# High weights of the last 64 inputs times low inputs: from eight full matmuls per output to seven and a share in two pairs of 64-row matmuls

## The chip, the cores and the metric

The kernel runs on one core of one Trainium2 chip. The metric is the device time of one execution in microseconds. Times and traces of the kernel before come from the hardware profiler; all times below are microseconds (us) unless marked ns.

## The reference: what is computed

Three parts follow each other, all in 32-bit floats. First a gated linear attention (mLSTM) over 2 batches, 8 heads, 768 steps and head size 40; its output, 1536 tokens of 320 numbers, goes into a gated layer and then into a two-layer one:

```
C = f_stab * C + i_stab * outer(v_t, k_t);  n = f_stab * n + i_stab * k_t
y_t = sigmoid(o_t) * (C q_t) / max(|n . q_t|, 1)          # 1536 x 320 over all steps
xn  = x / rms(x) * rms_g                                  # first layer's input
g   = xn @ w_gate;  val = xn @ w_val                      # 320 -> 1536 each
x   = (g * sigmoid(g) * val) @ w_out                      # 1536 -> 320
h   = x @ w_in                                            # 320 -> 2048
out = leaky_relu(h, 0.01) @ w_out2                        # 2048 -> 320
```

The weights are handed in as 64-bit floats and turned into 32-bit ones on the chip.

## The kernel before, in words

**Numbers as high and low parts.** TensorE (PE) multiplies in a shortened 32-bit format (fp32r). So each number of an input X and of a weight W is kept as a high part, rounded to that format, and a low part, the rest; a product is high times high, plus high times low, plus low times high. The input of a layer has 320 rows: two blocks of 128 and a last one of 64. The tile `X` holds six planes of 1536 token columns: planes 0, 1 and 2 are the high parts, 3, 4 and 5 the low ones. Planes 2 and 5 hold the last 64 inputs twice, in partitions 0 to 63 and again in 64 to 127. The weight tile `wA` of one block `f` has five planes: 0 and 1 high, 2 and 3 low, and plane 4 for the last 64 inputs, with the high weights in one half of the partitions and the low ones in the other. The halves alternate with the block's number (`weight_r`): an even block has its high weights in partitions 0 to 63, an odd one in 64 to 127.

**One output** of an up layer is 128 output features by 384 or 512 tokens, in one of the eight PSUM banks. The function `up` makes it with eight matmuls of 128 rows. The seventh is plane 4 times plane 2, which gives high times high and low times high for the last 64 inputs; the eighth is plane 4 times plane 5, which gives high times low, and low times low with it.

**Stages.** Attention runs in 12 tiles of 128 tokens (T = 0 to 11). Behind it the first layer's feature blocks 0 to 7 run in four token groups of 384 (`GA`), and blocks 8 to 11 and the whole second network in three groups of 512 (`GB`). `U.g.f.h` makes one output of block f for group g (h = 0 is the gate, tile name `g`, h = 1 the value, tile name `v`); T (tanh, ScalarE, ACT), E and M (products, VectorE, DVE), S (copy to the high part, ACT) and L (low part, DVE) follow; `D` and `DW` multiply down into 320 outputs (tiles `xa`, `xw`), `K` and `KW` add the result to `x2`, `FX` folds and `X` splits `x2` into the planes again. `H.g.f` makes an output of the second network (tile `h`), `R` applies the leaky relu (ACT, tile `u`), S and L split it, `O` multiplies down (tile `oa`), `OK` and `dO` keep and store. In attention `qk` makes the scores (tile `s`): for each head pair two matmuls of 40 rows, one in partitions 0 to 39 and one in 64 to 103, into two banks. `av`, `inn` and `kv` write column slices, `tp` transposes.

**What sets the order.** Nothing is scheduled when the kernel is built. The string `ORDER` lists the steps, `play` calls them in turn, and each engine and the DMA queue of SyncE (SP) run their instructions in that order; a step waits only where it needs data or a buffer. PSUM banks come from four tags of two banks each: `gv` (gates; outputs h with odd f), `s` (values of blocks 8 to 11; scores), `o` (outputs h with even f; xw of the third slice) and `acc` (sums). `a`, `r` and `b` convert weights on DVE and ACT, `id` are matmuls on constants that keep PE busy in attention.

Of the kernel before, what the change touches and what calls it, by code (L numbers as in the profile page):

```python
# [50 lines left out]
rec.0 wA.1 a.1 rec.1 r.2 dq.2 a.1 yr.0 id.1 mask.3.0 arg.3.0 r.2 id.1 r.2 qk.2 th.1 st.0 y1.1 de.2 dA.2.6 eq.2 ux.1.2
co.1.1.2 cv.1.1.2 cv.0.2.6 sq.0 y2.0.0 yr.1 wA.2 kv.1 dgb p.2.0 av.2.0 arg.2.1 y2.0.1 p.2.1 y2.0.2 k.2 sq.1 y2.1.0 a.2
y2.1.1 a.1 xn.0 a.2 arg.3.1 a.1 dq.3 qk.3 p.3.1 dq.4 cb.0 wB.1 a.2 xc.0 b.1 dsl y2.1.2 th.2 a.2 dr.2.6 da.4 mask.4.1
wA.4 xn.1 av.2.1 inn.2 y1.2 xc.1 id.1 st.1 abs.2 id.1 id.1 id.1 p.3.0 rec.2 tp.0 id.1 b.1 tp.1 dn.3 yr.2 dr.1.2
mask.4.0 dc.1.2 a.4 sq.2 b.1 y2.2.0 kv.2 xh.1 wR.3 th.3 de.3 dE.2.6 k.3 b.1 id.1 xh.0 xl.0 av.3.0 co.1.2.6 cv.1.2.6
xl.1 cb.1 y2.2.1 y2.2.2 r.3 qk.4 eq.3 av.3.1 inn.3 dv.1.2 xn.2 arg.4.0 xc.2 tp.2 abs.3 r.3 r.3 c.3 rec.3 dn.5 kv.3 a.4
xh.2 arg.4.1 xl.2 U.0.1.1 p.4.0 k.5 y1.3 da.5 a.4 st.3 U.0.1.0 cb.3 p.4.1 th.5 T.0.1 dn.4 th.4 mask.5.0 wA.3 yr.3 sq.3
a.4 E.0.1 mask.5.1 a.3 arg.5.1 dc.2.6 de.4 r.3 arg.5.0 y2.3.0 a.3 eq.4 M.0.1 av.4.0 av.4.1 inn.4 dq.5 qk.5 y2.3.1 y1.4
p.5.1 U.0.0.0 p.5.0 T.0.0 E.0.0 dv.2.6 U.0.0.1 M.0.0 da.6 mask.6.1 arg.6.1 de.5 wB.0 abs.4 dq.6 a.3 rec.4 mask.6.0
av.5.0 av.5.1 S.0.1 eq.5 y2.3.2 yr.4 S.0.0 inn.5 kv.5 abs.5 b.0 xn.3 rec.5 b.0 sq.4 y2.4.0 y2.4.1 arg.6.0 qk.6 L.0.1  # L60
p.6.1 U.0.2.0 p.6.0 U.0.2.1 T.0.2 E.0.2 c.2 y1.5 dq.7 b.0 c.5 st.5 qk.7 yr.5 y2.4.2 c.4 cb.5 sq.5 a.3 k.4 kv.4 id.1
xc.3 tp.3 xh.3 y2.5.0 y2.5.1 dq.8 xn.4 da.7 xc.4 M.0.2 wB.2 U.0.3.0 st.4 cb.4 y2.5.2 c.6 L.0.0 xn.5 xl.3 tp.4 xh.4
xl.4 U.0.3.1 S.0.2 xc.5 T.0.3 tp.5 xh.5 de.6 dn.6 av.6.0 E.0.3 xl.5 av.6.1 wB.3 M.0.3 L.0.2 eq.6 inn.6 abs.6 wA.5 b.0
b.3 U.1.0.0 T.1.0 E.1.0 U.1.0.1 M.1.0 U.1.1.0 da.8 U.1.2.0 b.3 mask.7.0 arg.7.0 p.7.0 dn.7 av.7.0 mask.7.1 arg.7.1
p.7.1 av.7.1 k.7 S.0.3 b.2 L.0.3 de.7 b.2 eq.7 S.1.0 b.2 inn.7 L.1.0 b.2 b.3 b.3 wB.4 rec.6 T.1.2 E.1.2 mask.8.1 a.5
da.9 mask.9.0 mask.9.1 b.4 qk.8 a.5 th.7 T.1.1 th.6 y1.6 D.0.0.2 E.1.1 D.0.0.1 K.0.0.1 U.1.2.1 M.1.2 U.1.1.1 arg.8.1
p.8.1 M.1.1 mask.8.0 D.0.0.0 S.1.1 L.1.1 yr.6 S.1.2 a.5 wA.7 U.1.3.0 a.5 L.1.2 arg.8.0 b.4 p.8.0 de.9 dq.9 kv.7 T.1.3
E.1.3 k.6 eq.9 kv.6 st.6 arg.9.1 cb.6 U.1.3.1 M.1.3 abs.7 a.7 dn.8 a.7 U.0.5.0 T.0.5 E.0.5 sq.6 qk.9 K.0.0.0 av.8.0
de.8 S.1.3 L.1.3 p.9.1 a.7 k.8 eq.8 av.8.1 rec.7 c.7 inn.8 th.8 abs.8 a.7 rec.8 U.0.4.0 wA.6 a.6 a.6 T.0.4 a.6 y2.6.0
y2.6.1 U.0.5.1 M.0.5 E.0.4 dq.10 dn.9 y1.8 yr.8 th.9 K.0.0.2 D.1.0.0 b.4 sq.8 U.0.4.1 st.7 a.6 U.0.6.1 M.0.4 wA.10  # L70
wB.6 b.6 b.6 S.0.4 L.0.4 y2.6.2 b.4 xn.6 U.0.6.0 cb.7 da.10 D.1.0.2 K.1.0.0 y1.7 D.1.0.1 k.9 T.0.6 mask.10.1 arg.9.0
wB.9 y2.8.0 yr.7 y2.8.1 E.0.6 p.9.0 M.0.6 y2.8.2 av.9.0 av.9.1 inn.9 b.6 K.1.0.2 kv.9 wB.5 b.5 b.5 abs.9 rec.9 c.9
st.9 S.0.5 kv.8 qk.10 mask.10.0 S.0.6 L.0.5 L.0.6 b.5 b.5 b.9 U.1.6.0 T.1.6 xn.8 xc.8 dn.11 c.8 st.8 xc.6 E.1.6 y1.9
yr.9 U.0.7.0 T.0.7 U.0.7.1 E.0.7 M.0.7 b.6 tp.6 cb.8 wB.7 b.7 b.7 b.7 b.7 K.1.0.1 tp.8 U.1.6.1 S.0.7 L.0.7 U.1.4.0
D.0.1.2 xh.6 M.1.6 xl.6 T.1.4 a.10 da.11 E.1.4 sq.7 y2.7.0 sq.9 y2.7.1 D.0.1.0 y2.7.2 mask.11.1 K.0.1.0 U.1.4.1 S.1.6
L.1.6 xh.8 xl.8 arg.10.0 y2.9.0 U.1.7.0 arg.10.1 p.10.1 T.1.7 E.1.7 D.0.1.1 dn.10 U.1.5.0 M.1.4 y2.9.1 p.10.0 xn.7
xc.7 y2.9.2 S.1.4 L.1.4 U.1.7.1 a.10 tp.7 M.1.7 de.10 eq.10 arg.11.1 cb.9 K.0.1.2 dq.11 qk.11 mask.11.0 xh.7 xl.7
T.1.5 av.10.0 av.10.1 E.1.5 inn.10 abs.10 rec.10 th.10 y1.10 yr.10 U.1.5.1 M.1.5 arg.11.0 S.1.5 S.1.7 U.2.2.0 L.1.5
T.2.2 L.1.7 U.2.1.0 T.2.1 E.2.1 sq.10 p.11.1 E.2.2 de.11 xn.9 D.1.1.0 K.1.1.0 U.2.1.1 M.2.1 U.2.2.1 S.2.1 M.2.2
U.2.0.0 L.2.1 T.2.0 E.2.0 D.1.1.2 K.1.1.2 wA.9 U.2.0.1 M.2.0 D.1.1.1 y2.10.0 S.2.2 y2.10.1 K.0.1.1 K.1.1.1 b.9 th.11  # L80
eq.11 S.2.0 L.2.0 U.2.3.0 T.2.3 L.2.2 U.2.3.1 xc.9 tp.9 xh.9 p.11.0 av.11.0 av.11.1 wR.5 E.2.3 M.2.3 S.2.3 y2.10.2
inn.11 L.2.3 D.2.0.1 abs.11 rec.11 y1.11 yr.11 sq.11 K.2.0.1 D.2.0.0 xn.10 D.2.0.2 y2.11.0 xc.10 xl.9 y2.11.1 y2.11.2
xn.11 xc.11 tp.10 tp.11 close U.2.4.0 a.10 a.10 wA.8 a.8 b.9 a.8 wR.4 xh.10 U.2.5.0 xl.10 wA.12 T.2.4 E.2.4 U.2.4.1
M.2.4 xh.11 xl.11 S.2.4 L.2.4 b.9 a.8 a.8 T.2.5 E.2.5 U.2.7.0 r.4 U.2.5.1 U.3.2.1 a.12 r.4 r.4 U.3.2.0 T.2.7 M.2.5
a.12 K.2.0.0 E.2.7 r.4 U.2.7.1 M.2.7 U.2.6.0 a.12 S.2.5 L.2.5 a.9 a.9 S.2.7 U.2.6.1 T.2.6 E.2.6 M.2.6 U.3.0.1 S.2.6
a.12 wA.14 K.2.0.2 U.3.0.0 L.2.6 L.2.7 D.2.1.2 a.9 T.3.2 E.3.2 wA.17 M.3.2 U.3.3.0 D.2.1.0 T.3.0 a.14 a.14 a.9 K.2.1.2
a.14 wB.8 a.14 E.3.0 M.3.0 r.5 wA.11 S.3.0 L.3.0 wR.6 a.17 T.3.3 D.2.1.1 E.3.3 U.3.3.1 r.5 S.3.2 M.3.3 a.17 S.3.3
L.3.3 K.2.1.0 L.3.2 a.17 a.17 wR.9 K.2.1.1 U.3.1.0 T.3.1 U.3.1.1 E.3.1 U.3.5.0 M.3.1 U.3.5.1 S.3.1 L.3.1 U.0.8.1 r.5
r.5 T.3.5 a.11 E.3.5 a.11 a.11 U.0.8.0 M.3.5 S.3.5 D.3.0.2 a.11 b.8 wA.13 a.13 b.8 b.8 b.8 a.13 U.3.4.0 T.3.4 L.3.5
a.13 U.3.4.1 E.3.4 K.3.0.2 M.3.4 D.3.0.1 T.0.8 r.6 K.3.0.1 r.6 E.0.8 M.0.8 a.13 D.3.0.0 r.6 wB.10 r.6 S.0.8 L.0.8  # L90
K.3.0.0 b.10 b.10 U.3.6.0 S.3.4 L.3.4 T.3.6 E.3.6 U.0.9.0 wB.11 b.11 b.10 U.3.6.1 T.0.9 E.0.9 wA.15 M.3.6 b.10 U.0.9.1
M.0.9 wR.7 DW.0.8 b.11 S.3.6 L.3.6 r.7 r.7 S.0.9 U.3.7.0 T.3.7 L.0.9 U.0.11.0 T.0.11 E.3.7 b.11 r.7 r.7 U.0.11.1
E.0.11 U.3.7.1 M.3.7 M.0.11 S.0.11 wB.13 U.0.10.0 b.11 L.0.11 wB.14 U.0.10.1 T.0.10 DW.0.9 b.13 E.0.10 b.13 a.15 a.15
a.15 M.0.10 U.2.10.0 wB.12 U.1.8.1 S.0.10 a.15 b.12 U.1.8.0 b.12 b.12 b.12 L.0.10 b.14 b.14 b.14 T.1.8 E.1.8 M.1.8
DW.0.10 DW.0.11 KW.0.1 KW.0.0 S.3.7 L.3.7 U.1.9.0 D.3.1.0 b.14 S.1.8 wB.17 L.1.8 KW.0.2 FX.0.0 FX.0.1 FX.0.2 wB.15
b.15 K.3.1.0 b.13 b.13 U.1.9.1 T.1.9 E.1.9 M.1.9 DW.1.8 U.1.10.1 U.1.11.1 S.1.9 wA.19 a.19 a.19 b.15 b.15 b.15 a.19
L.1.9 a.19 r.9 r.9 wA.18 a.18 a.18 U.1.10.0 T.1.10 a.18 E.1.10 T.2.10 M.1.10 DW.1.9 S.1.10 L.1.10 U.1.11.0 a.18
DW.1.10 wA.16 a.16 T.1.11 E.1.11 U.2.8.0 M.1.11 U.2.8.1 r.9 S.1.11 a.16 L.1.11 DW.1.11 r.9 a.16 a.16 U.2.11.1 KW.1.1
T.2.8 E.2.8 D.3.1.1 b.17 b.17 M.2.8 S.2.8 U.2.10.1 E.2.10 K.3.1.1 KW.1.0 wB.18 D.3.1.2 M.2.10 X.0.0 X.0.1 U.2.11.0
L.2.8 b.18 H.0.1 b.18 T.2.11 wR.8 H.0.0 E.2.11 M.2.11 b.18 b.18 wB.19 b.19 b.19 S.2.11 b.17 b.17 L.2.11 R.0.0 b.19  # L100
# [725 lines left out]
```

## Time and profile before

| | |
|---|---|
| median of 3 runs | 458.08 us (454.53 to 459.71) |
| profiled execution, its own time | 458.02 us |
| its span, first to last instruction | 456.2 us |
| PE busy, share of span | 441.6 us, 97% |
| DVE / ACT busy | 270.4 us / 232.3 us |
| mean granted TensorE clock | 0.977 |

The span is 1.8 us shorter than the execution's own time; the profiled execution is 0.06 us from the median. A busy PE counts a matmul from its start to its modelled end, and such ends overlap, so rates are read from the distance of starts, or from the chain of work that ended last, which gives each piece the time up to the next one's start.

### The profile page before, as it was taken

How to read it: one execution, taken by the hardware profiler on the slowest of the kernel's cores; microseconds unless marked ns; L12 is line 12 of the kernel's file. 1: busy time of each engine (PE TensorE's matmuls, PEld its weight loads, DVE VectorE, ACT ScalarE, POOL GpSimd, SP SyncE). 2: the span in 40 equal slices, each digit the busy share in tenths (PEclk: the TensorE clock that was granted, in tenths of full speed). 3: DMA queues.
4: the chain of work that ended last, by engine and by line, in shares of the span. 5: the costliest groups of instructions: out<-in, count | busy, mean ns of one | idle time of the engine just before them, and what ended most of it. 6: DMA issues, size and time to landing. Idle time of an engine off the chain costs nothing.

```text
span 456.2 us, 8986 instructions
## 1 busy us (share of the span) xinstructions
PE 441.6 (97%) x3566; PEld 393.6 (86%) x3568; DVE 270.4 (59%) x593; ACT 232.3 (51%) x549; POOL 53.1 (12%) x86
## 2 busy tenths in 40 slices
...
PEclk8579999999999999999999999999999999999999
DMA  7899894855810014331142110010101000010201
...
DMA packets 21034, 45.43 MB, mean 100 GB/s; under 512 B 2128, under 2 KB 9168, under 8 KB 20992
## 3 DMA queue, kind: packets, MB, share of 16 engines
...
q14 instruction: 14, 0.11, 0.1%
...
## 4 chain that ended last, share of the span: by engine, by line
PE 91%; DVE 4%; ACT 2%; issue 1%; ACTq 0%; DVEq 0%
PE h L568 20%; PE g L568 15%; PE v L568 14%; PE xa L631 10%; PE oa L699 6%; PE oa L697 6%; PE oa L698 6%; PE xw L649 5%; PE s L290 2%; PE o L350 1%; PE A L216 1%; PE busy L181 1%; PE o L360 1%; DVE w L337 1%; ACT w L306 1%
## 5 line engine op out<-in xcount | busy, mean ns | idle before, releaser
L568 PE MATMUL h<-X,wA 128*128 128x512 f32 x384 | 93.2, 395 | 0.0
L568 PEld LDWEIGHTS h<-X,wA 128*128 128x128 f32 x384 | 71.4, 188 | 15.7
L613 DVE TENSOR_TENSOR sl<-u,sh 128x512 fp32r<-128x512 f32 x48 | 32.8, 691 | 87.0 <-ACT sh L607 87.0
L568 PE MATMUL v<-X,wA 128*128 128x384 f32 (+1 forms) x352 | 73.7, 355 | 1.5 <-ACT X L458 0.7
L568 PE MATMUL g<-X,wA 128*128 128x384 f32 (+1 forms) x352 | 74.1, 355 | 0.0
L568 PEld LDWEIGHTS v<-X,wA 128*128 128x128 f32 x352 | 62.5, 188 | 6.6 <-DVE th L601 1.0
L568 PEld LDWEIGHTS g<-X,wA 128*128 128x128 f32 x352 | 62.2, 188 | 5.2 <-DVE th L597 0.6
L684 ACT ACTIVATE u<-h 128x512 f32<-128x512 f32 x48 | 28.6, 598 | 67.5 <-PE h L568 55.3
L698 PE MATMUL oa<-wB,sh 128*128 128x320 f32 x192 | 59.3, 309 | 0.0
L699 PE MATMUL oa<-wB,sl 128*128 128x320 f32 x192 | 59.3, 309 | 0.0
L697 PE MATMUL oa<-wB,sh 128*128 128x320 f32 x192 | 59.3, 309 | 0.0
L631 PE MATMUL xa<-sh,wB 128*128 128x384 f32 x160 | 45.6, 337 | 0.0
L607 ACT CAST sh<-th 128x384 fp32r<-128x384 f32 (+1 forms) x44 | 23.5, 542 | 36.4 <-DVE th L601 30.3
L698 PEld LDWEIGHTS oa<-wB,sh 128*128 128x128 f32 x192 | 36.0, 188 | 0.9
L697 PEld LDWEIGHTS oa<-wB,sh 128*128 128x128 f32 x192 | 36.0, 188 | 0.9
L607 ACT CAST sh<-u 128x512 fp32r<-128x512 f32 x48 | 29.6, 620 | 13.6 <-PE oa L698 12.6
L699 PEld LDWEIGHTS oa<-wB,sl 128*128 128x128 f32 x192 | 36.0, 188 | 0.0
L590 ACT ACTIVATE th<-g 128x384 f32<-128x384 f32 (+1 forms) x44 | 22.9, 520 | 25.3 <-PE g L568 20.9
L601 DVE SCALAR_TENSOR_TENSOR th<-th,v 128x384 f32<-128x384 f32 (+1 forms) x44 | 25.8, 589 | 12.6 <-PE v L568 11.4
L631 PE MATMUL xa<-sl,wB 128*128 128x384 f32 x96 | 32.3, 336 | 0.0
L597 DVE SCALAR_TENSOR_TENSOR th<-th,g 128x384 f32<-128x384 f32 (+1 forms) x44 | 25.8, 586 | 9.7 <-ACT th L590 9.7
L631 PEld LDWEIGHTS xa<-sh,wB 128*128 128x128 f32 x160 | 29.3, 188 | 0.4
...
## 6 DMA issues: line engine op xcount, KB each, us to landing
...
```

The costliest lines, as they stand in the source:

```text
L568: PE.matmul(dst, a, x, start=(i == 0), stop=(i == len(seq) - 1))
L590: A.activation(th, u[0], AF.Tanh, scale=0.5)
L597: V.scalar_tensor_tensor(out=u["t"], in0=u["t"], scalar=1.0, in1=u[0], op0=ALU.add, op1=ALU.mult)
L601: V.scalar_tensor_tensor(out=u["t"], in0=u["t"], scalar=0.5, in1=u[1], op0=ALU.mult, op1=ALU.mult)
L607: A.copy(u["h"], u["t"])
L613: V.tensor_tensor(u["l"], u["t"], u["h"].bitcast(F32), op=ALU.subtract)
L631: PE.matmul(xa, w, x, start=(k == 0), stop=(k == len(seq) - 1))
L649: PE.matmul(xas["w", g, i], a, x, start=(f == NE and k == 0), stop=(f == NF - 1 and k == len(seq) - 1),)
L684: A.activation(t, u[0], AF.Prelu, alpha=0.01)
L697: PE.matmul(dst, sh[:, ts], wb[:, 0:DM], start=first, stop=False)
L698: PE.matmul(dst, sh[:, ts], wb[:, DM:], start=False, stop=False)
L699: PE.matmul(dst, sl[:, ts], wb[:, 0:DM], start=False, stop=last)
```

## The change

Of an output's eight matmuls, `up` now issues seven where the block number is 8 or more (all outputs of blocks 8 to 11 and of the second network: 24 + 48 = 72 outputs of 512 columns); the outputs of blocks 0 to 7 keep eight. The eighth is left to `up_rest`: for four outputs together, from two blocks of different parity, it issues four matmuls of 64 rows, with only the half of plane 4 that holds the high weights and the same half of plane 5. They stand in the order even block, odd block, even, odd, so neighbours use different halves of the partitions and write different banks. The product low times low is no longer computed. Two new steps, `UR.g.p` (6 of them) and `HR.g.q` (12), call it, and only after them an output is complete.

```
-id.1 id.1 id.1 id.1 did cr id.1 id.1 dfg dig id.1 id.1 id.1 wR.1 dq.0 ms id.1 sf.0.1 sa.0.1 sf.1.2 id.1 sa.1.2 wA.0
...
+id.1 id.1 id.1 wR.1 id.1 id.1 cl id.1 id.1 dfg wR.0 id.1 dig id.1 r.1 did cr cr r.1 r.1 ms dq.0 wA.0 dn.2 dn.1 sf.0.1
...
-    def up(dst, w, m, cs):
+    def up(dst, w, m, cs, rest=True):
...
-        for i, (a, x) in enumerate(seq):
+        for i, (a, x) in enumerate(seq[:8 if rest else 7]):
             PE.matmul(dst, a, x, start=(i == 0), stop=(i == len(seq) - 1))
 
+    def up_rest(todo, cs):
+
+
+        for dst, key, m in todo:
+            p = slice(64 * (key % 2), 64 * (key % 2) + 64)
+            PE.matmul(dst, WA[key][p, 4, m * 128:(m + 1) * 128], X[p, 5, cs], start=False, stop=True)
...
-        up(u[h], WA[f], h, cs)
+        up(u[h], WA[f], h, cs, f < NE)
+
+    def u_rest(g, p):
+        cs, n = span(GB[g])
+        up_rest([(us[g, f][h], f, h) for h in range(2) for f in (NE + 2 * p, NE + 2 * p + 1)], cs)
...
-        up(us[g, NF + f][0], WA[NF + f // 2], f % 2, cs)
+        up(us[g, NF + f][0], WA[NF + f // 2], f % 2, cs, False)
+
+    def h_rest(g, q):
+        cs, w = span(GB[g])
+        up_rest([(us[g, NF + f][0], NF + f // 2, f % 2) for f in (4 * q, 4 * q + 2, 4 * q + 1, 4 * q + 3)], cs)
...
-        H=h_up, R=h_relu, O=out_down, OK=out_keep, dO=out_store,
+        H=h_up, HR=h_rest, UR=u_rest, R=h_relu, O=out_down, OK=out_keep, dO=out_store,
```

The string `ORDER` is another one from its first line on: it has the 18 new steps and two `id` fewer, and every other step as often as before, in another place. Three places follow. In the names the last number counts the tile, `x7` means seven instructions alike.

PE, where the outputs of blocks 10 and 11 for the third token group are made. Before, one of the four (`v2_11`) and the first rows of a piece of the down sum `xa` that follows it:

```order
L568 MATMUL v2_11_3543<-X_92,wA_11_2949 128x512 x8
L631 MATMUL xa3_1_1_3556<-sh3_4_3086,wB_4_1746 128x384
L631 MATMUL xa3_1_1_3556<-sl3_4_3088,wB_4_1746 128x384
L631 MATMUL xa3_1_1_3556<-sh3_4_3086,wB_4_1746 128x384
L631 MATMUL xa3_1_1_3556<-sh3_5_2972,wB_5_1954 128x384
```

Each of the four was complete with its eighth matmul, and `xa` pieces stood between them. Now the four stand together, seven matmuls each, with the four of 64 rows behind them, and then the down sum `xw` of the second group ends and that of the third begins:

```order
L569 MATMUL g2_10_3631<-X_92,wA_10_2602 128x512 x7
L569 MATMUL g2_11_3648<-X_92,wA_11_2889 128x512 x7
L569 MATMUL v2_11_3656<-X_92,wA_11_2889 128x512 x7
L569 MATMUL v2_10_3670<-X_92,wA_10_2602 128x512 x7
L576 MATMUL g2_10_3631<-X_92,wA_10_2602 128x512
L576 MATMUL g2_11_3648<-X_92,wA_11_2889 128x512
L576 MATMUL v2_10_3670<-X_92,wA_10_2602 128x512
L576 MATMUL v2_11_3656<-X_92,wA_11_2889 128x512
L660 MATMUL xw2_0_3687<-sh2_8_3618,wB_8_2835 128x512
```

All four banks of the tags `gv` and `s` are held until the last four matmuls are done; before, each output was complete by itself.

PE, at the start of the second network. Before:

```order
L568 MATMUL h0_1_3616<-X_92,wA_12_2733 128x512 x8
L568 MATMUL h0_0_3630<-X_92,wA_12_2733 128x512 x8
L568 MATMUL v2_9_3668<-X_92,wA_9_2694 128x512 x8
L568 MATMUL h0_2_3691<-X_92,wA_13_3012 128x512 x8
L568 MATMUL g2_9_3700<-X_92,wA_9_2694 128x512 x8
L568 MATMUL h0_4_3714<-X_92,wA_14_2832 128x512 x8
L568 MATMUL h0_3_3725<-X_92,wA_13_3012 128x512 x8
L568 MATMUL h0_5_3738<-X_92,wA_14_2832 128x512 x8
L697 MATMUL oa0_0_0_3752<-wB_12_3300,sh0_12_3735 128x320
```

Now:

```order
L569 MATMUL h0_3_3759<-X_92,wA_13_2963 128x512 x7
L569 MATMUL h0_0_3767<-X_92,wA_12_2780 128x512 x7
L576 MATMUL h0_0_3767<-X_92,wA_12_2780 128x512
L576 MATMUL h0_2_3706<-X_92,wA_13_2963 128x512
L576 MATMUL h0_1_3718<-X_92,wA_12_2780 128x512
L576 MATMUL h0_3_3759<-X_92,wA_13_2963 128x512
L569 MATMUL h0_6_3793<-X_92,wA_15_3060 128x512 x7
L569 MATMUL h0_7_3801<-X_92,wA_15_3060 128x512 x7
L569 MATMUL h0_5_3820<-X_92,wA_14_2828 128x512 x7
L569 MATMUL h0_4_3832<-X_92,wA_14_2828 128x512 x7
L576 MATMUL h0_4_3832<-X_92,wA_14_2828 128x512
```

The second four follow the first four with no other PE work between them. This is the one place where that is so; behind every other `UR` and `HR` stand one to seven steps DW, D or O.

ACT, in the same place, now (L699 is the leaky relu, L618 the copy to the high part, L674 the last part of FX, L682 the split of `x2` into X for the second group):

```order
L699 ACTIVATE u0_0_3782<-h0_0_3767 128x512
L699 ACTIVATE u0_1_3784<-h0_1_3718 128x512
L618 CAST sh0_12_3786<-u0_0_3782 128x512
L674 COPY x2_91<-x2_91 64x4x128
L618 CAST sh0_13_3791<-u0_1_3784 128x512
L699 ACTIVATE u0_3_3809<-h0_3_3759 128x512
L682 CAST X_92<-x2_91 128x4x3x128
L618 CAST sh0_15_3814<-u0_3_3809 128x512
L699 ACTIVATE u0_2_3818<-h0_2_3706 128x512
```

Before, the same FX and X stood ahead of the relu of output 2 as well, but PE went on with O steps of outputs that were ready:

```order
L607 CAST sh0_12_3735<-u0_0_3657 128x512
L663 COPY x2_91<-x2_91 64x4x128
L671 CAST X_92<-x2_91 128x4x3x128
L684 ACTIVATE u0_2_3780<-h0_2_3691 128x512
L607 CAST sh0_14_3782<-u0_2_3780 128x512
```

Of the four relus three are ahead of X now; the fourth, of output 2, frees the bank that output 4 takes.

## Rows read from the trace of the kernel before

**Rows 1.** The page: share of busy time of each engine; then in 40 slices.

```profile
PE 441.6 (97%) x3566; PEld 393.6 (86%) x3568; DVE 270.4 (59%) x593; ACT 232.3 (51%) x549; POOL 53.1 (12%) x86
...
PEclk8579999999999999999999999999999999999999
DMA  7899894855810014331142110010101000010201
```

**Rows 2.** Stretches: busy us (instructions) per engine, clock, DMA share, GB/s.

```profile
0.00:20.00 20.00, 19.17 (x116) 12.51 (x116) 11.63 (x29) 11.70 (x32) 9.48 (x23) 0.72 0.80 294
20.00:45.00 25.00, 18.87 (x429) 14.20 (x430) 22.63 (x66) 18.21 (x58) 9.98 (x16) 0.81 0.94 285
45.00:70.00 25.00, 22.07 (x428) 19.78 (x433) 23.05 (x56) 18.16 (x56) 13.56 (x20) 1.00 0.92 280
70.00:100.00 30.00, 30.00 (x415) 28.41 (x406) 23.00 (x56) 20.96 (x60) 11.63 (x18) 1.00 0.68 210
...
310.00:452.00 142.00, 142.00 (x789) 128.05 (x787) 42.52 (x74) 55.27 (x99) 0.00 (x0) 1.00 0.06 19
```

**Rows 3.** Chain that ended last, from 220 to 320 us: start, us, what.

```profile
222.25 1.84 PE xw L649 x8
...
312.80 7.47 PE h L568 x32
```

**Rows 4.** PE in order of time, 56 to 65 us: start, us, line, tile, shape, count.

```profile
56.51 1.16 PE L290 MATMUL s<-qkt 40*128 40x128 f32 x16
57.60 1.66 PE L568 MATMUL g<-X,wA 128*128 128x384 f32 x8
59.10 1.55 PE L568 MATMUL v<-X,wA 128*128 128x384 f32 x8
60.58 1.16 PE L290 MATMUL s<-qkt 40*128 40x128 f32 x16
...
62.49 0.49 PE L454 MATMUL tp<-consts,xn 128*128 128x128 f32 x3 [0.16 <-ACT xn L447]
62.74 1.65 PE L568 MATMUL g<-X,wA 128*128 128x384 f32 x8
64.23 0.49 PE L454 MATMUL tp<-consts,xn 128*128 128x128 f32 x3
64.47 0.42 PE L568 MATMUL v<-X,wA 128*128 128x384 f32 x1
```

**Rows 5.** PE in order of time, 115.5 to 117.5 us: transposes among up matmuls.

```profile
115.88 0.82 PE L454 MATMUL tp<-consts,xn 128*128 128x128 f32 x6
```

**Rows 6.** Chain, 49 to 55 us, and a group of 8 up matmuls behind another.

```profile
50.48 1.09 PE s L290 x16
51.57 1.60 PE g L568 x8
53.17 1.39 PE v L568 x8
```

**Rows 7.** Groups by shape: count, busy us, mean ns of one, idle before.

```profile
L568 PE MATMUL h<-X,wA 128*128 128x512 f32 x384 | 93.2, 395 | 0.0
...
L454 PE MATMUL tp<-consts,xn 128*128 128x128 f32 x36 | 5.8, 278 | 3.7 <-DVE X L462 2.5 <-DVE C L383 0.7 <-DVE xn L443 0.4
...
L684 ACT ACTIVATE u<-h 128x512 f32<-128x512 f32 x48 | 28.6, 598 | 67.5 <-PE h L568 55.3 <-DVE sl L613 12.1
L607 ACT CAST sh<-u 128x512 fp32r<-128x512 f32 x48 | 29.6, 620 | 13.6 <-PE oa L698 12.6
L671 ACT CAST X<-x 128x1536 fp32r<-128x1536 f32 x3 | 4.4, 1479 | 0.1
L663 ACT COPY x<-x 64x512 f32<-64x512 f32 x3 | 1.9, 618 | 0.8 <-DVE x L661 0.7
L590 ACT ACTIVATE th<-g 128x512 f32<-128x512 f32 x12 | 7.2, 598 | 9.0 <-PE g L568 7.6 <-DVE sl L613 1.1 <-DVE x L661 0.3
L597 DVE SCALAR_TENSOR_TENSOR th<-th,g 128x512 f32<-128x512 f32 x12 | 8.2, 685 | 3.4 <-ACT th L590 3.4
```

**Rows 8.** Chain, 0 to 80 us: two hand-overs, and PE's longest gap.

```profile
45.10 0.02 issue
45.12 0.57 DVE X L462
45.69 0.04 issue
45.73 1.50 PE v L568 x7
...
65.30 2.61 issue
67.92 0.56 DVE X L462
```

**Rows 9.** Waits, 0 to 70 us: engine, line <- releaser: us, times, longest.

```profile
DVE x L186 <- DMA x<-fg: 3.3, 1, 3.3
```

More of the change, by code (lines that the diff above doesn't have):

```diff
@@ L51 @@
[L51 to L100, printed above, removed]
@@ new lines @@
+y1.1 b.1 id.1 dq.2 y2.0.0 yr.1 ux.1.2 qk.2 p.2.1 p.2.0 mask.3.1 de.2 wA.4 arg.3.1 co.1.1.2 cv.1.2.6 kv.1 st.1 sq.1
+y2.1.0 dgb y2.0.1 y2.0.2 a.4 b.1 id.1 eq.2 av.2.0 da.4 cb.0 av.2.1 a.4 y2.1.1 inn.2 abs.2 rec.2 cv.1.1.2 dq.3 qk.3
+arg.3.0 mask.4.1 id.1 xn.0 y1.2 b.1 id.1 yr.2 mask.4.0 k.2 kv.2 sq.2 b.1 dn.4 dc.2.6 dn.3 de.3 k.3 eq.3 y2.1.2 xc.0
+wA.2 tp.0 xh.0 id.1 y2.2.0 th.3 dv.2.6 dE.2.6 p.3.0 p.3.1 a.4 xl.0 av.3.0 av.3.1 a.4 cb.1 inn.3 id.1 xn.1 y2.2.1
+y2.2.2 arg.4.0 a.2 wR.3 r.3 a.2 abs.3 kv.3 xc.1 rec.3 tp.1 dq.4 arg.4.1 r.3 qk.4 xn.2 xh.1 xl.1 id.1 xc.2 dn.5 tp.2
```

94 lines of the change are left out of this document (70 added, 24 removed).

## The prediction

> **What bounds the kernel now.** I read the engines' shares first: PE is busy 97% of the span, and its clock is full from the fourth slice of 40 on [rows 1]. Then the stretches: from 70 us on PE is busy all the time while DVE and ACT have slack (42.5 and 55.3 us of 142 at the end), but up to 70 us PE has gaps and DVE is the fuller one, 22.6 of 25 us and 23.1 of 25 [rows 2]. So there are two regimes. Behind 70 us the time is PE's list of matmuls, and only fewer or shorter PE gaps count; a wait of PE adds its full length. Ahead of 70 us the time is set by attention's work on DVE with its loads, and fewer matmuls would give nothing; the change removes none there.
>
> **What the removed matmuls are worth.** 72 eighth matmuls of 512 columns go. One costs the distance of starts, not its 395 ns [rows 7]: 32 in a row take 7.47 us, 233 ns each [rows 3]. That is 18 groups of four, 18 x 0.932 = 16.8 us of PE time.
>
> **What the pairs cost.** 72 matmuls of 64 rows come instead, in 36 pairs. The trace has such pairs: `qk` puts two 40-row matmuls on the two halves of the array, into two banks. Its 16 records take 1.09 us up to the next start (56.51 to 57.60) [rows 4]. Six full transposes with the same 128 columns end 0.82 us after their start, the last taking 0.28 [rows 7], so 0.108 us each [rows 5]; 16 of these one after another would be 1.73 us, 8 pairs at once 0.87. The pairs do run together. The seventh matmul and the pairs read the same planes as before, so I take a 512-column pair at one matmul's price, 233 ns, and a group of four at 0.466.
>
> But the switch to half-array work and back is not free. Up matmuls of 384 columns take 1.39 us for eight [rows 6]. Eight of them ahead of `qk` take 60.58 - 59.10 = 1.48 (0.09 more); `qk` takes 1.09 where 0.87 would do (0.22 more); the eight behind it take 59.10 - 57.60 = 1.50 (0.11 more) [rows 4]. Together 0.42 us for one trip there and back; if a pair takes 112 ns in place of 108 it is 0.39. I take 0.40. It is the geometry, not the number format: transposes in full 32-bit among the same up matmuls cost nothing beyond themselves (62.49 to 64.23 is 1.74 us for three transposes, 0.32, and eight matmuls, 1.39, within 0.03) [rows 4]. The Trainium skill, TensorEngine Tiling (Array Packing), Key Properties, says that a change of tiling mode, not merely of tile, drains the engine. By that rule each of the 18 steps pays twice, as the row on `qk` shows, though the page gives no price.
>
> So a group of four costs 0.466 + 0.40 = 0.87 us against 0.93: 0.066 us saved, and **18 x 0.066 = 1.2 us** in all, not the 8.4 us that half the matmuls suggest. Ends: with no switch cost -8.4 us, with pairs one after the other 18 x (0.932 + 0.40 - 0.932) = +7.2 us.
>
> **The waits that grouping adds.** An output is now complete only behind its 64-row matmul, and four banks are full at that time. Behind nearly every group PE has steps D, DW or O before it wants a bank again. The shortest cover is one DW (eight matmuls, 1.84 us [rows 3]) behind the first group for blocks 8 and 9 of the third token group: counted from the start of the first pair, the tanh can start at 0.44 and ends at 1.04, the product E ends at about 1.75 [rows 7], and PE wants the bank at 0.47 + 0.20 + 1.84 = 2.5. No wait; the next gate bank is free at about 3.9, behind three more DVE steps of 0.69, and is wanted at 4.1.
>
> The one group without cover is the first of the second network: the second four outputs follow at once. From the start s of the first pair: output 0 ends at s + 0.40 (mean 395 ns), its relu takes 0.60, so with hand-overs of 0.04 us [rows 8] its bank is free at about s + 1.08; without the wait PE would go on at s + 0.57. **0.5 us lost.** Output 4 needs the bank of output 2. On ACT stand ahead of its release two relus, a high part, the fold copy, a high part, a relu, the X split, a high part and the relu itself: 3 x 0.598 + 3 x 0.620 + 0.618 + 1.479 + 0.598 = 6.35 us from s + 0.44 [rows 7], so s + 6.83. PE would be there at s + 1.08 + 3 x 7 x 0.233 = s + 5.97. **0.9 us lost.** Nothing is gained for it elsewhere: the ACT work is the same in number. Bounds of both together: nothing, if the copies run when PE is still busy, and 1.4 plus one more X split, 1.5, if they slip. I take 1.4.
>
> Behind the last group of all, PE has seven O steps (12 matmuls each; the relus, copies and low parts of four outputs need some 6 us of ACT and DVE, the first O steps of ready outputs cover that), so the end is as before.
>
> **The new order ahead of 70 us.** Every step is there as often as before, less two `id`, which only fill PE. Steps on POOL, SP, DVE and ACT change places. The first load is now a weight of 256 KB ahead of the forget gates, at 294 GB/s 0.9 us [rows 2], and DVE, which waits 3.3 us for those gates [rows 9], has that weight's conversion to do in front of the scans; later attention loads stand within a few MB of where they stood, in a DMA queue that is 92 to 94% busy up to 70 us [rows 2]. As the stage is bound by the same DVE work, I cost it at nothing. What hides the moved loads is that work; where a load is late instead, DVE's loss comes in full. Bounds: the new order can save the one long gap of PE, 2.61 us while it waits for tile 4's low part [rows 8], and it can make another like it. So -2.6 to +2.6 us.
>
> **Sum.** 458.0 us (profiled execution, 0.1 from the median of the runs shown) - 1.2 + 1.4 + 0 = 458.2. With all of it uncertain by more than the odd tenth: **458 us**.
>
> **Rivals.**
> 1. *The switch costs little here.* For: the 0.40 comes from 128-column matmuls in another format, and a longer matmul could hide the weight load of the next. Against: both excesses are of the kind that doesn't shrink with columns: the wait for the array to empty and for the first weights after it. Fully free, 458.0 - 8.4 + 1.4 = 451.0 us; at half price (0.20) 18 x 0.266 = 4.8 saved, 454.6. The Trainium skill, TensorE: Matmul & The Clock Gate, Part 3 (measured speedup against the span model), counts a pack of tiles as one matmul plus some 4 ns per further tile and knows no price of entering or leaving; by it the 451 us would hold, and [rows 4] speak against it. Together with an order that saves the gap of 2.6 us, this is the way to be faster by over 1%. Chance 0.18.
> 2. *The pairs don't run together in this format* (slower). Each 64-row matmul then takes 233 ns and the switch comes on top: 18 x 0.40 + 1.4 = 8.6, 466.6 us. It turns slower from the point where a pair takes more than 0.27 us. For: the trace has no half-array matmul of the shortened format. Against: [rows 4] show pairs of the same geometry at once. Chance 0.06.
> 3. *The new order loses ahead of 70 us* (slower): a tile's load or a weight that comes too late where DVE has no slack, twice the gap of [rows 8], 458.2 + 5.2 = 463.4 us. For: DMA share above 90% and a load order that is new throughout. Against: every stretch behind 70 us has PE work in store. Chance 0.13.
> 4. Forecast, with -2.6 to +2.6 from attention and 0 to 2.9 for the waits: 455 to 462 us. Chance 0.63.
>
> That the change does nothing at all is no case: PE's order shows seven full and four half matmuls.
>
> Faster or slower by over 1% means below 453.5 or above 462.6; about 1% is what a measurement of this kernel tells from no change. Rival 1 is faster for most of its chance and the forecast's lower edge adds a little: 0.18. Slower: rivals 2 and 3 and a little of the forecast, 0.19. Same 0.63. The range, 453 to 463.5, leaves out the free switch, the serial pairs and the worse half of rival 3, under 2 in 10.
>
> **What would show it.** In the changed kernel's trace: the two matmuls of a pair start within 10 ns of each other, and the pairs 233 ns apart; from the first pair of a group to the first full matmul behind it some 0.75 us, not 0.47, and the full matmul ahead of it 0.09 longer. PE idle for about 0.5 us and 0.9 us ahead of outputs 6 and 4 of the first group, and nowhere else behind 80 us for over 0.3. The first time PE stays full within 2.6 us of 68.6. The forecast is wrong if a group of four takes 0.5 us in all (rival 1), if the halves start 233 ns apart (rival 2), or if PE has gaps of over 3 us ahead of 75 us (rival 3).

## The result: 0.8% slower

The changed kernel takes 462.05 us on the median of 20 runs (459.38 to 485.57), the kernel before 459.65 in 20 runs beside it (454.53 to 463.49). The ratio is 1.0077, with an interval of [1.0048, 1.0105]: 3.5 us, worked out from the ratio (2.4 us by the medians). Ratios leave out disturbed runs, so they need not agree with the medians to the last tenth. The forecast of 458 us is missed by 4, of which 1.6 us are the kernel before itself, 459.65 here and 458.08 in the three runs that the forecast started from. The time lies inside the range, but the forecast said no change, and the kernel got slower.

The profiled execution of the changed kernel took 465.3 us (span 463.5), above the median of its runs. So I compare durations in it, not its span. First the page, its busy shares and the granted clock in 40 slices.

```profile
PE 446.4 (96%) x3565; PEld 389.2 (84%) x3566; DVE 271.8 (59%) x593; ACT 229.8 (50%) x549; POOL 53.2 (11%) x86
...
PEclk9999997999999999999999999999999999999999
```

The clock now dips in the seventh slice, 70 to 81 us, where it was full before [rows 1]. Up to 36.9 us the 9s ahead of it, and the clock of 1.00 in the stretches below, are no reading: the trace of this execution has no record of the granted clock before that time, and the rows shown with run e7 below are as slow as those at half clock. The stretches of [rows 2] in the changed kernel (busy us and instructions per engine, clock, DMA share, GB/s) show the place:

```profile
0.00:20.00 20.00, 16.91 (x71) 11.49 (x71) 10.70 (x28) 10.32 (x28) 7.24 (x20) 1.00 0.84 293
20.00:45.00 25.00, 21.62 (x437) 15.65 (x438) 21.31 (x62) 17.75 (x59) 11.60 (x16) 1.00 0.87 259
45.00:70.00 25.00, 23.00 (x411) 19.97 (x411) 22.26 (x62) 19.48 (x59) 12.26 (x20) 1.00 0.87 265
70.00:100.00 30.00, 25.84 (x319) 24.17 (x322) 22.21 (x43) 17.66 (x53) 10.55 (x17) 0.89 0.60 209
310.00:452.00 142.00, 142.00 (x795) 123.79 (x795) 37.97 (x66) 55.31 (x104) 0.00 (x0) 1.00 0.05 15
```

Behind 100 us PE is full as before, but for one wait of 0.51 us shown below. Between 70 and 100 us, full in [rows 2], it is idle for 4.2 us. Here is that hole: a timeline of the changed kernel, 69.6 to 75.7 us (start, us, engine, line, operation, what ended the idle time before it). L444 is the normalization `xn` of tile 5, L455 the transposes that wait for it.

```profile
69.73 0.47 POOL L320 TENSOR_TENSOR C<-C,gdec 104x164 f32<-104x164 f32 x1 [2.80 <-ACT Cbd L390]
69.74 5.29 DVE L444 SCALAR_TENSOR_TENSOR xn<-y,sm,gb 128x320 f32<-128x320 f32 x1
...
70.16 1.30 POOL L315 TENSOR_TENSOR eb<-eb,qkt 128x512 f32<-128x512 f32 x1
71.41 0.64 POOL L311 TENSOR_SCALAR_AFFINE_SELECT Ab<-Ab 128x512 f32<-128x512 f32 x1
72.01 1.26 POOL L315 TENSOR_TENSOR eb<-eb,qkt 128x512 f32<-128x512 f32 x1
73.23 0.87 POOL L330 TENSOR_TENSOR Kt<-nat,aeu 128x160 f32<-128x160 f32 x2
74.05 0.64 POOL L311 TENSOR_SCALAR_AFFINE_SELECT Ab<-Ab 128x512 f32<-128x512 f32 x1
74.95 0.55 DVE L463 TENSOR_TENSOR X<-tp,X 128x384 fp32r<-128x384 f32 x1
...
75.55 0.48 PE L455 MATMUL tp<-consts,xn 128*128 128x128 f32 x1 [4.16 <-DVE X L463]
```

The normalization takes 5.29 us; for the other tiles this line takes 0.50 to 0.55, once 0.74. It begins within 10 ns of a run of seven POOL instructions and ends 0.34 us behind the last, at 75.03. The releaser named for the transposes (X L463) is only the next DVE instruction. The same stretch of the kernel before holds a smaller copy:

```profile
64.64 0.58 POOL L319 TENSOR_TENSOR C<-C,gdec 104x164 f32<-104x164 f32 x1 [1.08 <-ACT Cbd L389]
...
64.81 3.18 DVE L443 SCALAR_TENSOR_TENSOR xn<-y,sm,gb 128x320 f32<-128x320 f32 x1
65.19 1.29 POOL L314 TENSOR_TENSOR eb<-eb,qkt 128x512 f32<-128x512 f32 x1
...
66.43 1.22 POOL L310 TENSOR_SCALAR_AFFINE_SELECT Ab<-Ab 128x512 f32<-128x512 f32 x2
67.92 1.01 DVE L462 TENSOR_TENSOR X<-tp,X 128x384 fp32r<-128x384 f32 x2
```

This is the gap of 2.61 us in [rows 8], which I had put down to tile 4's low part. The Trainium skill, SBUF — State Buffer, Summary: rules for kernel authors, has the rule: a VectorE instruction with two SBUF inputs and a GpSimd instruction that reads SBUF exclude each other, and the later "**fully blocks** until the first finishes". The normalization has two such inputs, y and the gain. The rows agree on the block, but none of the POOL instructions is longer than 1.30 us; on its length the runs below decide.

Behind the hole the clock is at half its level, 1.2 GHz: granted 0.50 from 75 to 80 us. PE in order of time, in the changed kernel:

```profile
75.55 0.90 PE L455 MATMUL tp<-consts,xn 128*128 128x128 f32 x3 [4.16 <-DVE X L463]
76.38 0.77 PE L351 MATMUL o<-nat,w 128*32 128x41 f32 x32
76.93 1.31 PE L361 MATMUL o<-Cbd,eb 104*32 104x82 f32 x32
78.18 2.93 PE L569 MATMUL v<-X,wA 128*128 128x384 f32 x8
80.91 1.41 PE L569 MATMUL g<-X,wA 128*128 128x384 f32 x6
```

From the transposes to the gate matmuls it takes 80.91 - 75.55 = 5.36 us. In run e9 below the same four pieces run at the full clock; the first and the start of the gate matmuls there:

```profile
69.89 0.55 PE L456 MATMUL tp<-consts,xn 128*128 128x128 f32 x3 [1.50 <-DVE X L464]
...
72.94 1.55 PE L570 MATMUL g<-X,wA 128*128 128x384 f32 x8
```

That is 72.94 - 69.89 = 3.05, so half clock costs 2.3 us. In the profiled executions a gap of 2.48 us (before) or 2.45 (e1) left the clock full; gaps of 2.88 (e2) and of 4.14 to 5.32 (e3, e4, e11) were followed by a granted clock of 0.66 to 0.69 over 70 to 80 us.

The pairs and the waits, PE in order of time:

```profile
292.17 0.73 PE L576 MATMUL h<-X,wA 64*128 64x512 f32 x4
293.40 7.19 PE L569 MATMUL h<-X,wA 128*128 128x512 f32 x28 [0.51 <-ACT u L699]
300.52 0.73 PE L576 MATMUL h<-X,wA 64*128 64x512 f32 x4
301.19 0.41 PE L712 MATMUL oa<-wB,sh 128*128 128x320 f32 x1
```

The four take 0.73 us, and in all 18 groups the halves of a pair start 1 to 7 ns apart. Ahead of output 6 there is a wait of 0.58 us (0.51 of it idle), ahead of output 4 one of 0.40: two starts are 0.531 us apart at 298.17 and the next two 0.339, in place of 0.233 each.

### The profile page after: what moved, and what is told of

Its sections match the earlier page's. It is cut to its first block, busy times and chain, and to the rows that moved or that the text cites. A ratio compares the mean times of both kernels' runs of the same rounds, so it can differ in the third digit from the quotient of the medians.

```text
span 463.5 us, 8965 instructions
## 1 busy us (share of the span) xinstructions
PE 446.4 (96%) x3565; PEld 389.2 (84%) x3566; DVE 271.8 (59%) x593; ACT 229.8 (50%) x549; POOL 53.2 (11%) x86
## 4 chain that ended last, share of the span: by engine, by line
PE 84%; DVE 3%; ACT 3%; issue 1%; POOL 0%; DVEq 0%; ACTq 0%; POOLq 0%
PE h L569 16%; PE v L569 14%; PE g L569 14%; PE xa L642 10%; PE oa L712 6%; PE oa L713 6%; PE oa L714 6%; PE xw L660 5%; PE h L576 2%; PE s L291 1%; DVE xn L444 1%; PE o L351 1%; PE o L361 1%; PE tp L455 1%; PE o L373 1%
## 5 line engine op out<-in xcount | busy, mean ns | idle before, releaser
L569 PE MATMUL h<-X,wA 128*128 128x512 f32 x336 | 81.6, 396 | 0.6 <-ACT u L699 0.5
L569 PEld LDWEIGHTS h<-X,wA 128*128 128x128 f32 x336 | 62.3, 188 | 15.1 <-ACT u L699 1.5
L569 PE MATMUL v<-X,wA 128*128 128x384 f32 (+1 forms) x340 | 72.6, 358 | 0.3 <-issue 0.3
L569 PE MATMUL g<-X,wA 128*128 128x384 f32 (+1 forms) x340 | 71.0, 354 | 0.7 <-DVE th L608 0.7
L699 ACT ACTIVATE u<-h 128x512 f32<-128x512 f32 x48 | 28.3, 596 | 75.5 <-PE h L576 64.2
L569 PEld LDWEIGHTS v<-X,wA 128*128 128x128 f32 x340 | 61.3, 191 | 4.7 <-issue 0.6
L569 PEld LDWEIGHTS g<-X,wA 128*128 128x128 f32 x340 | 60.6, 189 | 5.5 <-DVE th L608 1.0
L712 PE MATMUL oa<-wB,sh 128*128 128x320 f32 x192 | 60.5, 315 | 0.0
L713 PE MATMUL oa<-wB,sh 128*128 128x320 f32 x192 | 59.3, 309 | 0.0
L618 ACT CAST sh<-th 128x384 fp32r<-128x384 f32 (+1 forms) x44 | 23.7, 542 | 28.8 <-DVE th L612 27.7
L618 ACT CAST sh<-u 128x512 fp32r<-128x512 f32 x48 | 29.3, 620 | 5.4 <-PE oa L713 3.9
```

The source lines that it names most:

```text
L569: PE.matmul(dst, a, x, start=(i == 0), stop=(i == len(seq) - 1))
L618: A.copy(u["h"], u["t"])
L699: A.activation(t, u[0], AF.Prelu, alpha=0.01)
L712: PE.matmul(dst, sh[:, ts], wb[:, 0:DM], start=first, stop=False)
L713: PE.matmul(dst, sh[:, ts], wb[:, DM:], start=False, stop=False)
```

## The experiments

Theory 1: the new order of the front (all steps up to `close`, where the attention ends) costs the time, and the change proper gains what was forecast. It has two parts that could each do it, 1a the blocked normalization and 1c a later beginning. Theory 2: the pairs or the order behind the attention cost it.

**e1 and e2: exchange the two halves of the order.**

```
e1: ORDER = before up to `close` (wA.9 -> wB.8, wR.5 -> wR.4), then the changed rest with UR, HR
e2: ORDER = after up to `close` (wB.8 -> wA.9, wR.4 -> wR.5), then the old rest, full eighth matmuls
```

> The order of the kernel before up to the step that closes the attention's pools, then the changed order with its pairs (in the first part two loads stand exchanged, wB.8 and wR.4 for wA.9 and wR.5, so that the buffers rotate as the second part wants). Theory 1, the loss comes from the new order of the front: the pairs save 18 x 0.077 = 1.4 us and the two waits at the second network's first groups cost 0.6 + 0.3, so the time is 0.5 us under the kernel before, 459.1 us on a median of 459.65 (ratio 0.999), and the transposes of tile 5 start at about 68.6 us as in the kernel before. Theory 2, the loss comes from the order behind the attention or from the pairs: about 462 us (1.006 or more), though the front is the old one.

> The reverse: the changed order up to the step that closes the attention's pools (the same two loads exchanged back), then the order of the kernel before with its eighth matmuls of 128 rows; no pair is left. Theory 1 (the front): the whole loss of the front without the 0.5 us that the rest gives back, 3.5 + 0.5 = 4.0 us over the kernel before, about 463.6 us (1.009), transposes of tile 5 at about 75 us. Theory 2 (what lies behind the attention): as the kernel before, 459.7 us (1.000).

Measured: e1 458.23 us, ratio 0.9967 [0.9936, 0.9999]; e2 464.17, ratio 1.0103 [1.0051, 1.0156]. Theory 2 falls on both. The new front costs 4.7 us (e2; by its interval 2.3 to 7.2) to 5.1 (1.0077 less 0.9967); the rest of the change gains. The start of tile 5's transposes, which I had expected at 68.6 and 75 us, is no good measure: it is 72.0 in e1 and 72.6 in e2, since in e1 the first up matmul came at 48.9 us, before at 45.1, with one and the same order there. The normalization of tile 5 takes 3.16 us in e1, as before, and 3.82 in e2.

**e3: full rows in the place of halves.**

```
-            p = slice(64 * (key % 2), 64 * (key % 2) + 64)
-            PE.matmul(dst, WA[key][p, 4, ...], X[p, 5, cs], start=False, stop=True)
+            PE.matmul(dst, WA[key][:, 4, ...], X[:, 5, cs], start=False, stop=True)
```

> The changed kernel, order and grouping kept, but the four matmuls of each group run over all 128 rows instead of 64 (what the halves leave out is added again). Theory 1: the pairs are a gain of 0.077 us for each of 18 groups, so this is 1.4 us slower than the changed kernel, about 463.4 us (1.008 to 1.011 of the kernel before). Rival, the changes of mode cost more than the trace shows: equal to the changed kernel or faster, 462 us or less. Each group of four should take 4 x 231 ns = 0.93 us in place of 0.855.

Measured: 464.18 us, 1.0107 [1.0060, 1.0153], that is 1.4 us over the changed kernel by the ratios, as expected (the intervals overlap; the trace carries the verdict). A group in e3, then one in the changed kernel, with the first full matmul behind each:

```profile
310.91 1.10 PE L575 MATMUL h<-X,wA 128*128 128x512 f32 x4
311.84 0.31 PE L711 MATMUL oa<-wB,sh 128*128 128x320 f32 x1
```

```profile
313.19 0.73 PE L576 MATMUL h<-X,wA 64*128 64x512 f32 x4
313.85 0.41 PE L712 MATMUL oa<-wB,sh 128*128 128x320 f32 x1
```

From the last full matmul ahead of a group to the second behind it, e3 takes 1.398 us with DW steps and 1.313 with O steps; the changed kernel takes 1.324 and 1.239. The difference is 0.074 us in either, times 18 = 1.3 us gained.

**e4: another order inside the group.**

```
-  ... for h in range(2) for f in (NE + 2 * p, NE + 2 * p + 1)
+  ... for f in (NE + 2 * p, NE + 2 * p + 1) for h in range(2)
-  ... for f in (4 * q, 4 * q + 2, 4 * q + 1, 4 * q + 3)
+  ... for f in range(4 * q, 4 * q + 4)
```

> The changed kernel with the four 64-row matmuls of a group in another order: both of one weight key, then both of the next, so that two neighbours read the same 64 rows and cannot run side by side. Theory: side by side, a pair takes the 231 ns of one matmul; in series it takes two, so each of the 18 groups loses two matmuls or more, 18 x 0.46 = 8.3 us, about 470.4 us (1.023 of the kernel before). Rival, that pairs gain nothing by running side by side: 462 us.

Measured: 464.36 us, 1.0107 [1.0054, 1.0161], and groups as short as ever: 0.67 us to the first full matmul behind them, starts 6 to 13 ns apart within a pair. My expectation was wrong. By the program's order the second of the four follows the first on the same 64 rows, and yet two start at once. The trace doesn't tell which two. I read it as the two halves each taking their own next instruction; that is an inference from the starts and not shown. The run says nothing on what pairs in series would cost.

**e5 and e6: keep GpSimd's run off the normalization**, in the changed kernel and in the kernel before (there C of tile 6 also goes behind `xc.5`).

```
-        A.copy(xn[:, DM:384], xn[:, 256:DM])
+        (G.tensor_copy if T == 5 else A.copy)(xn[:, DM:384], xn[:, 256:DM])
```

> The changed kernel, with one instruction moved: the 64-column copy of tile 5's normalized rows goes from ScalarE to GpSimd, where it stands ahead of the run of C, products, masks and K that in the changed kernel lay from 69.73 to 74.69 us over VectorE's normalization of tile 5. GpSimd can then begin that run only when the normalization is done. Theory 1a, the 5.29 us of that normalization are the run of GpSimd: it takes about 0.55 us, the transposes of tile 5 start 4 us earlier (71 to 72 us), TensorE's gap of 4.2 us there falls under 1 us, and the time is 3 to 4 us under the changed kernel, 458 to 459 us (0.997 to 1.000 of the kernel before). Rival 1b, what costs is the later start of the scans, 4 us already at 50 us: the normalization gets short, but the time stays at 461 us or more, because other tiles are late by as much.

> The kernel before (no pairs), with the same move of tile 5's 64-column copy to GpSimd, and C of tile 6 behind it. Theory 1a: the 3.18 us normalization of tile 5, at 64.81 to 67.99 us in the kernel before, is a block by GpSimd too, and not a wait for tile 4's low part. It falls to about 0.55 us, the gap of 2.61 us ahead of the transposes closes, and the time is about 2.6 us under the kernel before, 457.0 us (0.994). Rival: the transposes wait for something else that comes as late, the time stays within 1 us of the kernel before (0.998 to 1.002).

Measured: e5 459.61 us, 1.0003 [0.9966, 1.0039]; e6 457.26, 0.9953 [0.9919, 0.9987]. The normalization in e5, then in e6:

```profile
72.02 0.55 DVE L444 SCALAR_TENSOR_TENSOR xn<-y,sm,gb 128x320 f32<-128x320 f32 x1
...
72.71 0.24 POOL L448 COPY xn<-xn 128x64 f32<-128x64 f32 x1 [3.97 <-DVE xn L444]
...
73.52 0.49 PE L455 MATMUL tp<-consts,xn 128*128 128x128 f32 x3
```

```profile
65.38 0.55 DVE L443 SCALAR_TENSOR_TENSOR xn<-y,sm,gb 128x320 f32<-128x320 f32 x1
...
65.99 0.24 POOL L447 COPY xn<-xn 128x64 f32<-128x64 f32 x1 [1.85 <-DVE xn L443]
...
66.54 0.51 PE L454 MATMUL tp<-consts,xn 128*128 128x128 f32 x3
```

In both it takes 0.55 us and the transposes start without a wait. e5 lies just above the 458 to 459 us that theory 1a gave. The block is worth 2.2 us in the kernel before, as forecast for its gap, and 2.4 (medians) to 3.4 us (ratios) in the changed one. So theory 1a holds for the mechanism, but e5 doesn't get back the front's 5 us: by these ratios the growth of the block is worth some 1.2 us (with their intervals, 2.6 us either way), less than the 1.7 us of gap and 2.3 us of clock in the profiled execution. Nor does e5 show the block alone: in its profiled execution PE is idle again for 1.72 us from 81.23 us on, in the middle of 32 alike matmuls (L361, `o<-Cbd,eb`), and the profile names nothing that it waits for. The profiled executions of e7, e7b and e10, with the same front behind the beginning and the same copy, have such gaps of 0.56 to 1.14 us among these matmuls, those of e6 and e8, with the old front, none over 0.3 us.

**e9 and e11: lengthen GpSimd's run**, by the same two extra masks, which change no value a second time.

```
e9:   ... eq.6 da.8 av.6.1 +mask.8.0 +mask.8.0 mask.8.0 ... eq.7 ... k.6 ...
e11:  ... eq.6 da.8 av.6.1 mask.8.0 ... eq.7 +mask.8.0 ... k.6 +mask.8.0 ...
```

> The changed kernel with two masks more (the same one, for tile 8, which changes no value a second time) in the run of GpSimd that lay over tile 5's normalization. Theory 1a, the normalization is held until the whole run ends: it grows from 5.29 by two masks of 0.61 us to about 6.5 us, and the time by about 1.2 us and the half clock behind it, 463.3 to 464 us. Rival: VectorE is only held by the GpSimd instruction that runs when it starts, and gets its turn when that ends, and the 5.29 us have another cause: no growth, 462 us.

> The changed kernel with the same two extra masks as in the run with two more masks, but with other work of GpSimd between two of the same tile (behind the second product and behind K), so that none waits for the mask just ahead of it. In the run before, each of the masks in a row waited for the one ahead, GpSimd paused for 68 ns between them, and VectorE's normalization ended at that pause, after 2.63 us. Theory 1a': the normalization is held as long as GpSimd's instructions follow each other without a pause: here the run is unbroken and longer by 2 x 0.61 us, so it takes about 6.5 us, and the time is 1 to 2 us over the changed kernel, 463 to 464 us (1.009 to 1.011). Rival: the extra masks themselves let VectorE in, whatever their order: 2.6 us again, and 459.5 us.

Measured: e9 459.47 us, 0.9996 [0.9963, 1.0028]; e11 464.65, 1.0116 [1.0076, 1.0155]. VectorE and GpSimd, first in e9 and then in e11:

```profile
66.72 0.46 POOL L321 TENSOR_TENSOR C<-C,gdec 104x164 f32<-104x164 f32 x1 [2.78 <-ACT Cbd L391]
66.73 2.63 DVE L445 SCALAR_TENSOR_TENSOR xn<-y,sm,gb 128x320 f32<-128x320 f32 x1
...
67.14 1.29 POOL L316 TENSOR_TENSOR eb<-eb,qkt 128x512 f32<-128x512 f32 x1
68.39 2.17 POOL L312 TENSOR_SCALAR_AFFINE_SELECT Ab<-Ab 128x512 f32<-128x512 f32 x3
```

```profile
65.65 6.46 DVE L445 SCALAR_TENSOR_TENSOR xn<-y,sm,gb 128x320 f32<-128x320 f32 x1
...
65.65 0.46 POOL L321 TENSOR_TENSOR C<-C,gdec 104x164 f32<-104x164 f32 x1 [3.16 <-ACT Cbd L391]
66.07 1.29 POOL L316 TENSOR_TENSOR eb<-eb,qkt 128x512 f32<-128x512 f32 x1
...
70.55 1.22 POOL L312 TENSOR_SCALAR_AFFINE_SELECT Ab<-Ab 128x512 f32<-128x512 f32 x2
```

e9 went against both theories: more work on GpSimd, and the kernel got faster. Its three masks in a row each wait for the one ahead; the first ended at 69.02 and the second began at 69.09, and in that pause of 69 ns VectorE got in. Between the instructions ahead of it there is no pause: each begins 41 to 47 ns before the end of the last. e11 was made to tell this from the masks themselves. With as much work and no pause the normalization takes 6.46 us where 6.5 was expected, and the time rises by 1.8 us over the changed kernel (1.0116 against 1.0077; the intervals overlap, those of e9 and e11 don't). So VectorE can be held for a whole run of GpSimd instructions, and not for one. By the rule of the Trainium skill quoted above it would be 1.30 us at most.

That an unbroken run always holds it to the end does not follow. In e2 it got in ahead of the K step (L329, tile `Kt`), though that step begins 35 ns before the end of the product `eb` ahead of it, and a mask follows without a pause:

```profile
68.28 3.82 DVE L443 SCALAR_TENSOR_TENSOR xn<-y,sm,gb 128x320 f32<-128x320 f32 x1
...
71.71 1.11 POOL L329 TENSOR_TENSOR Kt<-nat,aeu 128x160 f32<-128x160 f32 x2
```

The two K matrices take 1.11 us there, 0.87 in the changed kernel, where the same step did not let VectorE in. The normalizations of other tiles got in ahead of a K step in the same way, after 1.55 us in e5 (at 47.20 us) and 0.83 in e7b (at 45.83). What decides it, the runs don't show.

e9 also prices the growth of the block in another way than e5. Its gap is 1.50 us in place of 4.16, no half clock follows, and it is 3.7 us faster than the changed kernel by the ratios (2.0 us either way). Its gap is also 1.0 us shorter than the 2.48 us of the kernel before, so the growth from there and the half clock behind it are worth some 2.7 us.

**e7, e7b and e10: the beginning.** PE's first blocks in the changed kernel, then in the kernel before:

```profile
7.09 0.79 PE L214 MATMUL A<-consts_r 128*128 128x512 f32 x1 [2.33 <-ACT consts_r L739]
7.81 2.07 PE L217 MATMUL A<-x,consts 16*128 16x128 f32 x8
```

```profile
5.72 0.49 PE L213 MATMUL A<-consts_r 128*128 128x512 f32 x1
6.14 1.15 PE L216 MATMUL A<-x,consts 16*128 16x128 f32 x8
```

The constants come later, behind two weight loads, and all four such blocks take 2.07 us, where before the first two took 1.15. The third of the kernel before takes 2.07 us too, from 9.34 us on at a granted clock of 0.50. The first value products start at 22.33 us, before at 19.23. Over the profiled executions with the new front (the changed kernel, e2, e3, e4, e5, e9, e11) they start at 21.7 on the mean and the first up matmul at 49.7; with the old front (before, e1, e6, e8) at 18.6 and 46.0.

```
e7, e7b: e5 with ORDER's first 71 steps as before, the rest as in the changed kernel
e10:     e5 with  did dfg dig  ahead of  wR.1 wR.0,  and the three first r.1 behind  sa.1.2
```

> The changed kernel with the copy on GpSimd (459.6 us), and the first 71 steps (loads, scans, rows of the first tile, up to the first scores) in the order of the kernel before. Theory 1c, what is left of the front's loss lies in that beginning: the scans end 2 us earlier, the first up matmuls start about 2 us earlier, and the time is 1.5 to 2 us under the kernel with the copy alone, about 457.8 us (0.996). Rival: the beginning is hidden by what follows, and the time stays at 459 to 460 us (0.999 to 1.001).

> The kernel with the old beginning (first 71 steps) once more, since its first timing left open whether it beats the kernel with the copy alone: its median was 459.6 us over all runs, its ratio 0.9956. Theory 1c: 457.8 us, ratio 0.994 to 0.998. Rival: 459 to 460 us, 0.999 to 1.001.

> The changed kernel with the copy on GpSimd (459.6 us), and of the beginning only this is put back: the constants and the two gate inputs are loaded ahead of the first weights, and the first weight conversion stands behind the first scans. Theory 1c, the late beginning is these loads: the constants are cast at about 3 us instead of 6.2, the scans of the first columns end about 2 us earlier, the first value products start at about 20 us instead of 22.2, and the time is 1.5 to 2 us lower, about 457.8 us (0.996 of the kernel before). Rival: what follows hides it, 459 to 460 us (0.999 to 1.001).

Measured: e7 459.61 us, 0.9956 [0.9917, 0.9995]; the same kernel as e7b 460.02, 1.0007 [0.9965, 1.0048]; e10 458.90, 0.9975 [0.9942, 1.0008]. Against e5 (1.0003) this is inconclusive: nothing to 2.2 us gained, each with 2.3 us or more either way by the intervals. In e10 the constants are cast at 2.84 us as expected, but the value products start at 21.3, not 20. In e7b PE waits 1.39 us for the score products on DVE that the other order puts there. So the later beginning is in the traces, and no edit of its first steps alone brought it back reliably.

**e8: the parts that gained, together.** The old front with the copy on GpSimd, the changed rest with pairs, and

```
-  psum(f"h{g}_{f}", "gv" if f % 2 else "o")
+  psum(f"h{g}_{f}", "gv" if f % 2 else "s" if (g, f) in ((0, 4), (0, 6)) else "o")
```

with `R.0.4` moved up behind `R.0.6`.

> The order of the kernel before in front and the changed order with pairs behind it (458.2 us measured), with the copy on GpSimd and with outputs 4 and 6 of the second network's first group in another PSUM tag, one that is free there, so that they wait for no relu. By the terms: 2.6 us for the block and 0.9 us for the two waits, about 454.7 us (0.989 of the kernel before). If the waits go elsewhere (to the first output block, which then needs that tag) only the 2.6 us are won: 455.6 us (0.991).

Measured: 454.67 us, 0.9892 [0.9849, 0.9935], against both kernels the fastest. The first group of the second network in e8:

```profile
279.52 0.73 PE L576 MATMUL h<-X,wA 64*128 64x512 f32 x4
280.18 7.04 PE L569 MATMUL h<-X,wA 128*128 128x512 f32 x28
287.15 0.73 PE L576 MATMUL h<-X,wA 64*128 64x512 f32 x4
```

The next group begins 7.63 us behind this one, in the changed kernel 8.36. So 0.73 us of the two waits are gone. A smaller one has come in their place: output 5, the third of this group, now waits 0.24 us for the relu of output 3 (two starts 0.368 us apart and the next two 0.338).

## Why the prediction missed

**The bound** held: behind 100 us PE is full, and only its list and its waits count there.

**The pairs** held, with their small gain. The price of the mode switch was right: forecast 0.40 us a trip and 0.066 us gained per group, measured 0.39 and 0.074; 1.2 us against 1.3. Its parts lay elsewhere: the pairs start 0.335 us apart, not 233 ns, and the first full matmul follows 0.66 us behind the first pair, not 0.75. Rivals 1 and 2 fall on the same rows: a group takes 0.86 us with its switches, not 0.5 in all, and the halves start together.

**The waits** were right in place and half right in size: forecast 0.5 and 0.9, in the trace 0.58 and 0.40, of which e8 got back 0.73. The second was over-sized from both ends: the nine instructions on ACT take 5.90 us and not 6.35, since most of them begin some 0.1 us before the end of the one ahead, and PE arrives 6.24 us behind the first pair and not 5.97.

**The new order ahead of 70 us** is the step that failed: "As the stage is bound by the same DVE work, I cost it at nothing", with bounds of -2.6 to +2.6 us. It cost about 5. Two things were wrong. The gap of 2.61 us was read as a wait "for tile 4's low part" because the chain names that instruction behind it. The instruction ahead, on the same engine, was the normalization at six times its usual length, and a look at one instruction's own time in that window would have shown it. In the changed kernel it takes 5.29 us, and the gap is 4.16. An order that moves POOL's steps then changes how long DVE is held, though both have the same work as before. And I costed the first 20 us by DVE's work when PE's blocks there, the constants that they wait for and the speed they run at moved too.

Rival 3 had the sign and nearly the size (463.4), and its mark, a gap of over 3 us ahead of 75 us, came true. Its reason did not hold there: at tile 5 no load was late. In the beginning the constants were, but e10, which loads them first, got back no more than 1.3 us, with 2.3 either way.

The sum by the runs: pairs -1.3, waits +1.0, front +4.7 (e2) is 4.4 us, against 3.5 measured. Of the front, the block's growth and the half clock behind it are worth 1.2 us by e5 and e6 and 2.7 by e9, each with 2 us or more either way. **What stays open** is the rest. Counted from the 4.7 it is 2 to 3.5 us. Counted from e9 it is about 1 us: pairs, waits and a gap 1.0 us shorter than in the kernel before make -1.3 us, and e9 measured -0.2. In the traces the new front is late at the first up matmul, 3.7 us on the mean over executions that scatter by 5 to 6 us, and e7, e7b and e10 got back between nothing and 2.2 us. Which of the moved steps ahead of 50 us it is, and how much, these runs don't settle.
